# Attention and MLP on one core: the first batch's steps in another order, with zero products between them

## The chip, the cores and the metric

The kernel runs on one core of a Trainium2 chip. The metric is the device time of one execution in microseconds (us). Before the change it is 412.58 us, the median of three runs (412.34 to 412.92).

A core has five engines that each work through their own instructions in program order and wait for one another by semaphores: TensorE (PE, matrix products, with its weight loads PEld beside it), VectorE (DVE), ScalarE (ACT, exponentials and other activations), GpSimd (POOL) and SyncE (SP, which here only issues DMAs). DMAs are also issued by POOL and ACT. All DMAs of the core share 16 DMA engines.

## The reference

```python
rmsnorm = lambda x, g: x / np.sqrt(np.mean(x * x, -1, keepdims=True) + 1e-6) * g
q_n, k_n = rmsnorm(q, g_q), rmsnorm(k, g_k)          # q, k, v: 8 x 12 x 448 x 64
scores = q_n @ k_n.transpose(0, 1, 3, 2) / 8
attn = exp(scores - max) / (sum + 1e-9)
x = (attn @ v).transpose(0, 2, 1, 3).reshape(3584, 768)
out = gelu_tanh(x @ w_in) @ w_out                    # w_in 768 x 2048, w_out 2048 x 768
```

Eight batches; inputs and output are float32, the kernel multiplies in bfloat16.

## The kernel before, in words

Each batch has 12 heads, worked in six pairs (`hp` 0 to 5), and three chunks `c` of two pairs each (`hp = 2c + j`). For each chunk the raw q and k come in by DMA (`loads(b, c)`, lines 114 to 149, issued by SP: two for q, four for k). Then squares (`square`, L174), sums of the squares (`total`, L203, DVE), the inverse root (`rsqrt`, L209 and L212, an Ln and an Exp on ACT), the product with it (`normed`, L226), a transpose on PE (`trans`, L238 for q and L245 for k) and a copy out of PSUM (`place_q` L251, `place_k` L257). Scores are k against q (L324, and L310 for the 64 left-over keys of two pairs together), the exponential is on ACT (L331), and from it come on PE the row sums (`o` with `ones`) and the products with v (`ox` with `vb`, `vr`), both L370. The sums are turned into inverses on DVE (`recip_in`, `recip`, `recip_out`, L377 to L385), and `pair_x` (L395) gives the attention's output. The first layer of the MLP is `mm1` (L412, tiles `hh` and `h`) with `gelu` (L421), the second is `mm2` (L441).

From the second batch on, one batch's second-layer products fill PE between the next batch's attention steps. In the first batch there is nothing to fill with, and what every engine does in which order is written out by hand as a string `FRONT` (L761) that `front(step)` (L669) carries out one step after another. Every engine keeps the string's order for its own instructions. The steps are named so (`:A`, `:D`, `:P` say ACT, DVE or POOL):

- `sq0` to `sq5`, `sk0` to `sk5`: squares of pair number i; `tq`, `tk`: their sums; `rs`: Ln and Exp; `nq`, `nk`: products; `tpq`, `tpk`: transposes; `cq`, `ck`: copies out.
- `gcol`, `shift`: the gains g_q g_k and the constant under the exponential, with four zero products.
- `s0` to `s20`, `e0` to `e20`: 21 tiles of scores and their exponentials. Tile 3 (and 10, 17) holds the left-over keys of both pairs of a chunk, so it needs both pairs' q and k. Two PSUM buffers hold scores, three after step `U`.
- `sa`, `sb`: row sums in two halves; `xa`, `xb`: products with v in two halves; `st`, `rc`, `rb`, `xt`: inverses and `pair_x`.
- `y`n: n zero products of 224 columns; `z`m: m zero products of 448 columns into pair 0's sum bank, which its sum later overwrites. Both call `idle` (L214). The string before has one `y3` and no `z`.
- `v0` to `v2`: DMAs of batch 0's v from POOL (`v0` is the large part `vb`, `v1` and `v2` the left-over keys `vr`); `V` the same of batch 1; `w0` to `w3`: four parts of w_in; `o0` to `o3`: four parts of w_out, all from POOL. `L11`: `loads(1, 1)`, and so on.
- Batch 1's own preparation has capitals: `Sq`, `Sk`, `Tq`, `Tk`, `Rs`, `Nq`, `Nk` (`Nk01`: chunk 0, j 1), `Tp`, `Cq`, `Ck`.
- `mb`, `ma`, `mc`, `md`: first-layer products of batch 0; `g`: their gelu. `GELU` and `EXP` load activation tables.

Ahead of `FRONT` stand `loads(0, 0)`, `loads(0, 1)`, `loads(0, 2)`, `loads(1, 0)` (L604 to L608) and 20 zero products of 448 columns.

Of the kernel before, what the change touches and what calls it, by code (L numbers as in the profile page):

```python
# [8 lines left out]
F32 = mybir.dt.float32  # L9
# [7 lines left out]
def kernel(  # L17
# [12 lines left out]
    B, H, S, D = q.shape  # L30
# [8 lines left out]
    P = 112  # L39
    NQ = S // P  # L40
# [70 lines left out]
    def head(c, j):  # L111
        return 2 * c + HP * j

    def load_q(b, c):
        t = rawqk.tile([P, CH, NQ, D], F32, tag="rawq", name="rawq")
        raws["q", b, c] = t
        return [
            lambda j=j: nc.sync.dma_start(  # L118
                t[:, 2 * j:2 * j + 2],
                q[b, head(c, j):head(c, j) + 2].rearrange("h (p t) d -> p h t d", t=NQ),  # L120
            )
            for j in range(2)
        ]
# [481 lines left out]
    nc.scalar.preload_act_table_set(EXP_SET)  # L605
    loads(0, 1)
    loads(0, 2)
    loads(1, 0)  # L608
    nc.vector.memset(eps, 1e-6)
    nc.vector.memset(ones, 1.0)  # L610
    nc.vector.memset(rows, 1.0)
# [57 lines left out]
    def front(step):  # L669
        what, _, eng = step.partition(":")  # L670
        name, i = what.rstrip("0123456789"), what[len(what.rstrip("0123456789")):]
        i, eng = int(i or 0), ENG.get(eng)
        c, j = i // 2, i % 2
        n = name[-1]
        if name in ("sq", "sk"):
            square(0, c, n, eng, ("pair", j))
        elif name in ("tq", "tk"):
            total(0, c, n, j)
        elif name == "rS":
            rsqrt(0, i, slice(0, 30))  # L680
        elif name == "rs":
            rsqrt(0, c, slice(14 * j, 14 + 16 * j))
        elif name in ("nq", "nk"):
            normed(0, c, n, j, eng)
        elif name in ("tpq", "tpk"):
            tps[n, i] = trans(0, i, n, ps_t_tiles, name)
        elif name == "cq":
            place_q(0, i, tps["q", i], eng)
        elif name == "ck":
            place_k(0, i, tps["k", i], eng)  # L690
        elif name == "U":
            third()
        elif name == "gcol":
            gains()
        elif name == "shift":
            shifts()
        elif name == "s":
            exps[i] = scores(0, *TILES[i])
        elif name == "e":
            exps[i]()  # L700
        elif name == "z":
            hp, m = divmod(i, 100)
            if hp not in sums_at:
                sums_at[hp] = bank()
            idle(m, sums_at[hp][:, :S])
        elif name == "y":
            idle(i, ps_m.tile([128, 512], F32, tag="mm", name="w")[:, :S // 2])
        elif name in ("sa", "sb"):
            pair_products(0, i, 0, sums_at.get(i), "ab".index(n))
        elif name == "su":  # L710
            pair_products(0, i, 0, sums_at.get(i))
        elif name == "xp":
            pair_products(0, i, 1, ps_m.tile([128, 512], F32, tag="mm", name="ox"))
        elif name == "st":
            recip_in()
        elif name == "rc":
            recip()
        elif name == "rb":
            recip_out(i)
        elif name in ("xa", "xb"):  # L720
            pair_products(0, i, 1, ps_m.tile([128, 512], F32, tag="mm", name="ox") if n == "a" else None,
                          "ab".index(n))
        elif name == "xt":
            pair_x(0, i)
        elif name == "v":
            load_v(0, i)
        elif name == "w":
            w_in_part(i, NW)
        elif name == "V":
            load_v(1, i)  # L730
        elif name == "o":
            w_out_part(i // 2, slice(i % 2 * nf // 2, (i % 2 + 1) * nf // 2))
        elif name == "L":
            loads(*divmod(i, 10))
        elif name in ("Sq", "Sk"):
            square(1, i, n, eng)
        elif name in ("Tq", "Tk"):
            total(1, i, n)
        elif name == "Rs":
            rsqrt(1, slice(0, 2))  # L740
        elif name in ("Nq", "Nk"):
            normed(1, i // 10, n, i % 10, eng)
        elif name == "Tp":
            tps["Q", i] = trans(1, i, "q", ps_o, "o")
            tps["K", i] = trans(1, i, "k", ps_m, "mm")
        elif name in ("Cq", "Ck"):
            (place_q if n == "q" else place_k)(1, i, tps[n.upper(), i], eng)
        elif name in ("GELU", "EXP"):
            nc.scalar.preload_act_table_set(EXP_SET if name == "EXP" else GELU_SET)
        elif name == "mb":  # L750
            mm1(0, [0, 1], [i], act=False)
        elif name in ("ma", "mc", "md"):
# [22 lines left out]
    for step in FRONT.split():
        front(step)
# [159 lines left out]
```

## Time and profile before

| what | value |
|---|---|
| median of three runs | 412.58 us |
| the profiled execution's own time | 413.83 us |
| its span, first to last instruction | 412.1 us |
| mean granted TensorE clock | 0.992 of full speed |
| busy share of the span: PE, DVE, ACT, POOL | 98%, 67%, 72%, 32% |
| chain of waits that ended last, PE's share | 95% |
| read from memory, written | 45.61 MB, 11.01 MB |

A row of the timeline gives the start in us from the span's start, the duration, the engine, the line, the operation, the tile written and those read, sizes, and how many instructions of the kind stand in a row. In brackets is the engine's idle time before it and whose signal ended it. A row of stretches gives for a window the busy us (and number of instructions) of PE, PEld, DVE, ACT and POOL, then the granted clock, the busy share of the DMA engines and GB/s. A row of a group gives busy us, mean ns of one, idle time before. Squares of batch 0 are written into the space of the tile `g`, so they appear as `g<-rawq` and `g<-rawk`. Matmul durations include the drain of the array, so a product's price is read from the distance of two starts.

### The profile page before, as it was taken

How to read it: one execution, taken by the hardware profiler on the slowest of the kernel's cores; microseconds unless marked ns; L12 is line 12 of the kernel's file. 1: busy time of each engine (PE TensorE's matmuls, PEld its weight loads, DVE VectorE, ACT ScalarE, POOL GpSimd, SP SyncE). 2: the span in 40 equal slices, each digit the busy share in tenths (PEclk: the TensorE clock that was granted, in tenths of full speed). 3: DMA queues.
4: the chain of work that ended last, by engine and by line, in shares of the span. 5: the costliest groups of instructions: out<-in, count | busy, mean ns of one | idle time of the engine just before them, and what ended most of it. 6: DMA issues, size and time to landing. Idle time of an engine off the chain costs nothing.

```text
span 412.1 us, 10085 instructions
## 1 busy us (share of the span) xinstructions
PE 403.7 (98%) x4207; PEld 243.5 (59%) x4207; DVE 274.3 (67%) x454; ACT 296.2 (72%) x398; POOL 131.8 (32%) x144
## 2 busy tenths in 40 slices
PE   8799999999999999999999999999999999999996
PEld 3344555566655666557655666556655575556664
DVE  4899739899899638884678747786488633783010
ACT  5797987969988587767977778785976558774300
POOL 7689000234500942037500745019310460000000
PEclk9699999999999999999999999999999999999999
DMA  8999995999981689229981399616991161210022
GB/s 191 227 235 228 203 196 141 227 227 192 213 145 38 139 176 207 66 52 176 222 140 41 78 203 171 136 40 145 171 145 40 23 112 40 72 46 2 2 77 78
DMA packets 97870, 54.21 MB, mean 132 GB/s; under 512 B 63776, under 2 KB 94368, under 8 KB 97824
## 3 DMA queue, kind: packets, MB, share of 16 engines
q1 hardware_dynamic: 71392, 41.69, 43.4%
q0 software_dynamic: 26112, 11.80, 22.5%
q8 instruction: 33, 0.54, 0.6%
q10 hardware_dynamic: 320, 0.07, 0.1%
q14 instruction: 13, 0.11, 0.1%
HBM read 45.61 MB, written 11.01 MB: 137 GB/s over the span
## 4 chain that ended last, share of the span: by engine, by line
PE 95%; SPq 2%; DMA 1%; DVE 0%; ACT 0%; issue 0%; ACTq 0%; DVEq 0%
PE o L441 36%; PE hh L412 31%; PE o L370 11%; PE sc L324 8%; PE h L412 5%; PE sc L310 1%; DMA rawq<-in_q_dram 1%; PE ox L370 1%; SPq L143 1%; SPq L118 1%; SPq L136 1%; PE tp L245 0%; PE o L477 0%; PE tp L238 0%; ACT ex L331 0%
## 5 line engine op out<-in xcount | busy, mean ns | idle before, releaser
L441 PE MATMUL o<-wout,g 128*64 128x384 bf16 (+1 forms) x1648 | 160.6, 327 | 0.0
L331 ACT ACTIVATE ex<-sc,shift 128x896 bf16<-128x896 f32 x144 | 136.1, 1011 | 1.3 <-PE sc L324 1.3
L412 PE MATMUL hh<-xT,win 128*64 128x448 bf16 (+1 forms) x1260 | 133.8, 353 | 0.0
L441 PEld LDWEIGHTS <-g 128*64 128x64 bf16 (+1 forms) x1648 | 96.2, 109 | 58.3 <-issue 14.8
L412 PEld LDWEIGHTS <-win 128*64 128x64 bf16 (+1 forms) x1440 | 95.4, 109 | 49.9 <-issue 3.2
L421 ACT ACTIVATE g<-hh 128x896 bf16<-128x896 f32 x56 | 50.1, 919 | 44.5 <-PE hh L412 44.4
L203 DVE TENSOR_REDUCE ss<-sq 128x14 f32<-128x896 f32 (+4 forms) x45 | 47.9, 1080 | 32.4 <-ACT sq L186 19.9
L454 ACT COPY osb<-o 128x384 f32<-128x384 f32 x50 | 24.2, 483 | 47.8 <-PE o L441 47.8
L788 POOL COPY mark<-es 1x1 bf16<-1x1 bf16 x8 | 1.8, 225 | 162.9 <-DVE es L345 158.5
L377 DVE STREAM_TRANSPOSE st<-o 128x448 f32<-128x448 f32 x48 | 31.1, 648 | 23.6 <-PE o L370 23.2
L324 PE MATMUL sc<-qT,kT 64*128 64x448 bf16 (+1 forms) x372 | 39.6, 360 | 1.7 <-DVE kT L264 1.3
L345 DVE TENSOR_TENSOR es<-ex 128x896 bf16<-128x896 bf16 x42 | 26.8, 637 | 12.0 <-ACT ex L331 12.0
L226 POOL TENSOR_TENSOR nrmq<-rawq,rinv 112x512 bf16<-112x512 f32 x33 | 34.0, 1043 | 0.0
L226 POOL TENSOR_TENSOR nrmk<-rawk,rinv 128x512 bf16<-128x512 f32 (+1 forms) x33 | 31.1, 957 | 4.2 <-ACT rinv L212 4.2
L385 DVE STREAM_TRANSPOSE rb<-rc 128x448 f32<-128x448 f32 x48 | 31.0, 645 | 1.6
L370 PE MATMUL o<-ex,vb 128*64 128x448 bf16 x252 | 30.9, 352 | 0.0
L279 DVE TENSOR_SCALAR kT<-kT,gcol 128x896 bf16<-128x896 bf16 x19 | 21.1, 1108 | 11.7 <-DMA kT<-nrmk 11.7
L343 DVE TENSOR_TENSOR es<-es,exr 64x896 bf16<-64x896 bf16 x42 | 25.9, 617 | 2.4 <-ACT exr L331 1.0
L345 DVE TENSOR_TENSOR es<-es,ex 128x896 bf16<-128x896 bf16 x42 | 25.5, 608 | 2.3 <-ACT ex L331 0.3
L395 DVE TENSOR_TENSOR xT<-o,rb 128x448 bf16<-128x448 f32 x42 | 25.8, 615 | 1.4 <-PE o L370 0.9
L188 POOL TENSOR_TENSOR sq<-rawq 112x1024 f32<-112x1024 f32 x9 | 17.0, 1893 | 28.4 <-DMA rawq<-in_q_dram 25.0
L324 PEld LDWEIGHTS <-kT 64*128 64x128 bf16 (+1 forms) x372 | 10.9, 99 | 24.6 <-issue 18.1
(83 smaller groups left out, 349.4 us busy)
## 6 DMA issues: line engine op xcount, KB each, us to landing
rawq<-in_q_dram SPq DMA_DIRECT2D x48, 224.0 KB, 4.4
rawk<-in_k_dram SPq DMA_DIRECT2D x48, 192.0 KB, 4.6
vb<-in_v_dram POOLq DMA_DIRECT2D x8, 576.0 KB, 10.1
win<-in_moe_w_in_dram POOLq DMA_DIRECT2D x4, 768.0 KB, 14.1
wout<-in_moe_w_out_dram POOLq DMA_DIRECT2D x4, 768.0 KB, 20.4
out_dram<-osb SPq DMA_DIRECT2D x7, 336.0 KB, 4.3
out_dram<-osb SPq DMA_DIRECT2D x8, 288.0 KB, 2.7
out_dram<-osb SPq DMA_DIRECT2D x8, 240.0 KB, 2.6
```

The costliest lines, as they stand in the source:

```text
L203: nc.vector.reduce_sum(stat(ssq[b % 3], b, c, n, j), view(n, sqs[n, b, c], j), axis=AX.X)
L226: eng.tensor_mul(dst.rearrange("p t a d -> p a t d"), view(n, raws[n, b, c], j), r.to_broadcast(list(r.shape) + [D]),)
L324: nc.tensor.matmul(sc[o, a, :S], kT[r, c, 4 * j + t, o], qT[b][r, hp], start=True, stop=True,)
L331: nc.scalar.activation(dst, sc[:, :, :S], AF.Exp, scale=scale, bias=shift)
L343: nc.vector.tensor_add(es[p], es[p], exrs[b, hp // 2][p])
L345: nc.vector.tensor_add(es, ex[:, 0] if t == 1 else es, ex[:, t])
L370: nc.tensor.matmul(o[a * D:(a + 1) * D], w(a), e[:, a], start=(i == 0), stop=(i + 1 == len(steps)),)
L377: nc.vector.transpose(oas["st"].rearrange("p a b -> p (a b)"), oas[0])
L385: nc.vector.transpose(oas["rb", hp], oas["rc"].to_broadcast([128, S // 32, 32]))
L412: nc.tensor.matmul(h[i * m:(i + 1) * m, j, :S], win[:, c // 2 + NCH * (c % 2), f * 128 + i * m:f * 128 + (i + 1) * m], xT[b][:, c], start= ...
L421: nc.scalar.activation(g[:, fs[0]:fs[0] + len(fs), (b % 2) * S:(b % 2 + 1) * S], hs1[fs[0]][:, :, :S], AF.Gelu_apprx_tanh)
L441: nc.tensor.matmul(o[j * m:(j + 1) * m, :HD], g[:, f, i * 128 + j * m:i * 128 + (j + 1) * m], wout[:, f, half * HD:(half + 1) * HD], start ...
```

## The change

Three things change. `loads(1, 0)` is no longer issued ahead of `FRONT` but at a step `L10` in it, and a new step `H10` sets one element of its q tile to zero on POOL, for which the DMA into that tile has to wait. The string `FRONT` is another: squares and products change engine (`sq0` from ACT to POOL, `sq1` from POOL to DVE, `sk2` from ACT and `sk3` from POOL to DVE, `sq2` from ACT to POOL, `sq4` from POOL to ACT, `nq0` and `nk0` swap DVE and POOL, `cq1` from DVE to ACT; in batch 1 `Sk1`, `Sk2`, `Sq2` from ACT to POOL and `Sq0` from POOL to ACT, where it stands ahead of `e20`), `v1`, `v2` and `v0` come earlier on POOL, `w0` later, and there are more zero products: `y4`, `z5`, `y3`, `y1`, `y5`, `y1`, `y4`, `y1`, `z2`. What is computed stays the same.

```diff
+    def raw_q(b, c):
+        if ("q", b, c) not in raws:
+            raws["q", b, c] = rawqk.tile([P, CH, NQ, D], F32, tag="rawq", name="rawq")
+        return raws["q", b, c]
+
     def load_q(b, c):
-        t = rawqk.tile([P, CH, NQ, D], F32, tag="rawq", name="rawq")
-        raws["q", b, c] = t
+        t = raw_q(b, c)
...
     loads(0, 2)
-    loads(1, 0)
...
+        elif name == "H":
+
+            eng.memset(raw_q(*divmod(i, 10))[:1, 0, 0, :1], 0.0)
...
     FRONT = """
-        sq0:A sk0:P gcol tq0 tk0 sq1:P rs0 sk1:A nq0:P v1 nk0:D shift tq1 tk1 sq2:A tpq0 tpk0 v2
-        v0 sk2:A rs1 sq3:A cq0:D ck0:D tq2 s0 e0 y3 s1 nk1:D nq1:D L11 e1 tpk1 tpq1 s2 sk3:P w0
-        tq3 tk2 rs2 e2 ck1:D cq1:D s3 e3 sa0 s4 sk4:P tk3 nq2:D nk2:D rs3 tpk2 tpq2 s5 sb0 tk4
-        ck2:D cq2:D nq3:D st0 e4 nk3:P e5 s6 sk5:P L12 e6 tpk3 tpq3 s7 e7 s8 sa1 s9 sb1 xa0 e8
-        sq4:P sq5:P w1 rc0 cq3:D rb0 ck3:D tq4 tk5 rs4 e9 xb0 s10 st1 xt0 rc1 rb1 tq5 e10 sa2
-        s11 e11 rs5 nk4:P nq4:P w2 nk5:P nq5:P xa1 xb1 sb2 s12 e12 s13 tpk4 tpq4 xt1 st2 ck4:D
-        cq4:D rc2 xa2 e13 rb2 sa3 xb2 s14 tpk5 tpq5 s15 e14 xt2 ck5:D cq5:D sb3 e15 U s16 s17
-        xa3 xb3 s18 w3 o0 Sk0:P e16 st3 rc3 rb3 e17 xt3 e18 s19 sa4 xa4 sb4 xb4 Tk0 st4 rc4 s20
-        mb0 mb1 mb2 mb3 sa5 e19 e20 o1 Sq0:P Sq1:P V0 rb4 GELU xt4 Tq0 xa5 sb5 xb5 st5 V1 V2 o2
-        o3 Sk1:A rc5 rb5 ma1 mc0 mc1 xt5 md0 ma2 md1 mc2 md2 Tq1 Tk1 g0 EXP md3 Rs0 g1 Nk00:D
-        Nq11:D Nq00:D Tp0 md4 Cq0:A g2 Sq2:A g3 Nk10:D Nk01:D Nq01:D Ck0:D Tp1 md5 Sk2:A Tq2 Tk2
-        Nk11:D Nq10:D Ck1:A g4 Cq1:A g5 md6 md7 g6 g7 md8 g8
+        sq0:P sk0:P tq0 tk0 gcol rs0 sq1:D sk1:A v1 v2 tq1 nq0:D nk0:P tk1 shift tpq0 tpk0 y4 v0
+        rs1 sq3:A ck0:D cq0:D s0 e0 s1 z5 y3 nk1:P sk2:D nq1:D H10:P sq2:P e1 tpk1 s2 y1 tpq1 y5
+        y1 y4 tq3 tk2 e2 ck1:D sk3:D tq2 L10 cq1:A rs2 s3 e3 tk3 nk2:D nq2:D rs3 y1 z2 s4 sa0 s5
+        sb0 tpq2 tpk2 nq3:D st0 ck2:D cq2:D e4 sk4:P nk3:P e5 s6 sq5:P w0 w1 sk5:P e6 sq4:A tpk3
+        tpq3 s7 sa1 s8 sb1 xa0 e7 e8 s9 xb0 rc0 tk4 rb0 tq4 ck3:D cq3:D st1 xt0 e9 rs4 s10 tk5
+        tq5 rc1 rb1 L11 L12 e10 s11 xa1 sa2 rs5 e11 nq4:P nk4:P nq5:P nk5:P xb1 sb2 s12 tpq4
+        tpk4 xt1 e12 st2 ck4:D cq4:D s13 xa2 sa3 e13 rc2 rb2 s14 tpq5 tpk5 s15 xb2 e14 ck5:D
+        cq5:D xt2 sb3 e15 U s16 s17 xa3 xb3 s18 Sk0:P w2 w3 e16 st3 rc3 rb3 e17 xt3 e18 s19 sa4
+        sb4 xa4 s20 xb4 mb0 mb1 mb2 Tk0 st4 rc4 mb3 sa5 e19 Sq0:A o0 Sq1:P o1 V0 V1 Sk1:P V2 rb4
+        e20 GELU o2 xt4 Tq0 sb5 xa5 xb5 st5 Sk2:P o3 Sq2:P rc5 rb5 mc0 ma1 xt5 md0 mc1 ma2 md1
+        mc2 md2 Tk1 Tq1 g0 EXP md3 Rs0 g1 Nk00:D Nq00:D Nq01:D Tp0 md4 Nk10:D Nk11:D Nk01:D g2
+        g3 Cq0:D Ck0:A Tp1 md5 Nq11:D Tq2 Cq1:D Nq10:D Tk2 Ck1:A g4 g5 md6 md7 g6 g7 md8 g8
 """
```

## The prediction

> **What bounds the kernel now.** I read the page's slices first, then the stretches by clock, then the order of time on each engine. In the slices TensorE (PE) stands at nine tenths from about 15 us to the last slice; what can move the end is how early its dense work begins.
>
> ```profile
> 10.00:15.00 5.00, 2.31 (x18) 1.06 (x19) 5.00 (x11) 3.50 (x8) 3.69 (x4) 0.90 1.37 219
> 15.00:20.00 5.00, 5.00 (x29) 1.79 (x28) 4.21 (x10) 4.32 (x7) 2.74 (x3) 0.50 1.34 235
> 20.00:25.00 5.00, 4.59 (x41) 2.03 (x41) 4.42 (x10) 4.66 (x7) 4.10 (x5) 0.92 1.20 233
> ```
> The last columns are granted clock, DMA share and GB/s. PE is busy for 2.31 of 5 us in the first stretch, and the clock falls to half for the next: 0.90, 0.50 and 0.92 put the half clock from 14.0 to about 20.8 us. The DMA engines are full all along.
>
> PE in order of time (start, duration, line, what; in brackets the idle time before it):
> ```profile
> 1.16 6.91 PE L217 MATMUL w<-zeros 128*128 128x448 bf16 x20 [1.16 <-DVE zeros L81]
> ...
> 8.13 0.93 PE L217 MATMUL w<-zeros 128*128 128x448 bf16 x4
> ...
> 9.10 0.33 PE L245 MATMUL tp<-ident,nrmk 128*128 128x128 bf16 x3
> 10.73 0.36 PE L324 MATMUL sc<-qT,kT 64*128 64x448 bf16 x2 [1.30 <-DVE kT L264]
> 11.02 0.46 PE L217 MATMUL w<-zeros 128*128 128x224 bf16 x3
> ...
> 13.36 0.37 PE L238 MATMUL tp<-ident,nrmq 112*128 112x112 bf16 x4 [1.05 <-DVE nrmq L226]
> ...
> 14.80 0.88 PE L310 MATMUL sc<-qT,kT 64*64 64x448 bf16 x4 [0.78 <-DVE kT L264]
> ...
> 36.34 0.55 PE L370 MATMUL o<-ex,ones 128*64 128x448 bf16 x4
> 36.72 0.55 PE L370 MATMUL ox<-ex,vb 128*64 128x448 bf16 x4
> 37.20 7.74 PE L412 MATMUL hh<-xT,win 128*128 128x448 bf16 x40
> 44.82 0.37 PE L238 MATMUL tp<-ident,nrmq 112*128 112x112 bf16 x4
> ...
> 47.52 0.36 PE L238 MATMUL tp<-ident,nrmq 112*128 112x112 bf16 x4
> ```
> PE waits for VectorE (DVE) until 14.8; from 37.20 the 40 products of the first layer take 0.19 us each (7.74 us without a gap). Zero products raise the clock too: the first twenty average 0.35 us, those at 8.13 take 0.23 with their drain.
>
> ScalarE (ACT), the 21 exponentials of batch 0 and their neighbours:
> ```profile
> 10.54 0.61 ACT L186 ACTIVATE g<-rawq 112x512 f32<-112x512 f32 x1
> 11.13 1.91 ACT L331 ACTIVATE ex<-sc,shift 128x896 bf16<-128x896 f32 x2
> 14.39 0.31 ACT L209 ACTIVATE lg<-ss,eps 128x14 f32<-128x14 f32 x1 [1.36 <-DVE ss L203]
> ...
> 14.85 0.99 ACT L331 ACTIVATE ex<-sc,shift 128x896 bf16<-128x896 f32 x1
> 15.74 1.00 ACT L331 ACTIVATE exr<-sc,shift 128x896 bf16<-128x896 f32 x1
> ...
> 17.11 1.01 ACT L331 ACTIVATE ex<-sc,shift 128x896 bf16<-128x896 f32 x1
> ...
> 32.25 2.82 ACT L331 ACTIVATE ex<-sc,shift 128x896 bf16<-128x896 f32 x3
> ...
> 46.47 1.06 ACT L186 ACTIVATE sq<-rawq 112x1024 f32<-112x1024 f32 x1
> ```
> The same engine between 10 and 35 us, one group:
> ```profile
> L331 ACT ACTIVATE ex<-sc,shift 128x896 bf16<-128x896 f32 x18 | 17.3, 1006 | 1.3 <-PE sc L324 1.3
> ```
> One exponential follows another by 0.89 us (14.85 to 15.74), an rs step puts in 0.46 (14.39 to 14.85). e3 starts at 15.74, e20 ends at 35.07. Between them ACT is full but for 1.3 us in which scores came late, most of it at half clock. So batch 0 is set by when e3 starts and by ACT behind it. PE is then 1.3 us behind ACT (its last sums start at 36.34).
>
> **The change part by part.** DVE and GpSimd (POOL) need rows of their own:
> ```profile
> 9.96 0.38 DVE L255 COPY qT<-tp 128x448 bf16<-128x448 bf16 x1
> 10.26 0.41 DVE L264 TENSOR_SCALAR kT<-tp,gcol 128x384 bf16<-128x384 bf16 x1
> ...
> 11.78 1.53 DVE L226 TENSOR_TENSOR nrmq<-rawq,rinv 112x512 bf16<-112x512 f32 x1
> 13.23 1.13 DVE L203 TENSOR_REDUCE ss<-g 112x8 f32<-112x512 f32 x2
> ...
> 15.57 0.67 DVE L226 TENSOR_TENSOR nrmq<-rawq,rinv 112x512 bf16<-112x512 f32 x1
> 16.17 0.54 DVE L226 TENSOR_TENSOR nrmk<-rawk,rinv 128x384 bf16<-128x384 f32 x1
> ...
> 43.01 0.56 DVE L226 TENSOR_TENSOR nrmk<-rawk,rinv 128x384 bf16<-128x384 f32 x1 [1.62 <-ACT rinv L212]
> ```
> ```profile
> 8.43 1.48 POOL L159 DMA_DIRECT2D vr<-in_v_dram  x2
> 9.90 1.06 POOL L153 DMA_DIRECT2D vb<-in_v_dram  x1
> 11.71 1.04 POOL L188 TENSOR_TENSOR g<-rawk 128x512 f32<-128x512 f32 x1 [0.76 <-DMA rawk<-in_k_dram]
> ...
> 30.42 1.70 POOL L188 TENSOR_TENSOR sq<-rawk 128x896 f32<-128x896 f32 x1
> ...
> 33.01 3.75 POOL L188 TENSOR_TENSOR sq<-rawq 112x1024 f32<-112x1024 f32 x2
> ```
> The same DVE product takes 0.67 us at 15.57 and 1.53 at 11.78, while POOL's square of 11.71 runs; POOL lost nothing. Two-input products of DVE and POOL shut each other out, and here the one that stood waiting went ahead of DVE's next product. The Trainium skill, "SBUF — State Buffer", section "Who interferes with whom", says that a DVE tensor_tensor with both inputs in SBUF contends with GpSimd's reads and that the later one blocks fully. The trace agrees (1.53 against 0.67); the rule speaks against this change, which gives both engines more such products.
>
> *Before e0.* The first square goes to POOL (1.04), sq1 to DVE (no DVE square is in the trace: 0.60 by the product's spacing from 15.57 to 16.17, at most POOL's 1.04), and tq1 now comes ahead of nq0. PE's zero products still hold the first transposes until 9.10, so this is hidden: nq0 on DVE waits for POOL's nk0 and ends near 8.3. What DVE no longer has ahead of cq0 is one reduction, 0.60: I get ck0, cq0 ending at 10.2 and s0 at 10.27 instead of 10.73. But sq3 stands ahead of e0 on ACT and waits for its load. With 0.61 for sq3, e0 starts at about 10.85 instead of 11.13.
>
> *v sooner.* The issues (1.48 and 1.06) move from 8.43 and 9.90 to about 5.4 and 7.7. Landing of k's and q's loads here, the q half for sq3 (issued 5.34), v's large part, and the last k of batch 1:
> ```profile
> DMA to landing us min/median/max: 4.8/4.8/4.8
> ```
> ```profile
> DMA to landing us min/median/max: 10.7/10.7/10.7
> ```
> ```profile
> DMA to landing us min/median/max: 11.5/11.5/11.5
> ```
> sq3's load lands at 10.14; v's small pieces now share its last microsecond, which I price at 0.1 (0 if they start as late after the issue as the 3 us that other loads need, 0.7 if they take every other packet from 7 on). v's large part landed at 20.6; its first reader xa0 moves from 22.84 to about 20.4. I take no wait; a landing at 21.5 would cost about 0.5 at e9, 0 if v gains its two microseconds.
>
> *DVE from 10.2 to e3.* Behind cq0 stand sk2 (new on DVE), nq1, tq3, tk2, ck1, sk3 (new), tq2, then rs2 on ACT, which is queued ahead of e3. sk2 waits for POOL's nk1 (9.62 to 10.66) and ends at 11.1. POOL's sq2 waits by then and goes first, as at 11.71, so nq1 ends at 12.5 (unblocked 11.7). tq3 and tk2 (1.1 by the 13.23 row), ck1 (0.4), sk3 (0.60), tq2 (0.6) give 15.2; rs2 starts at 15.26, e3 at 15.73. That is where it was. The two squares taken over by DVE eat what was won before; ACT waits about 1.2 us ahead of rs2 with cq1 hidden in it. **Below and above:** 14.87 if DVE keeps the turn at 11.1, 16.5 if POOL's sk4 also gets in ahead of sk3.
>
> *Zero products.* y4, z5, y3, y1, y5, y1, y4, y1, z2: 23 short ones against 3, and 7 long ones. At 0.1 us (11.02 row: three to 11.41) and 0.19 they add 2.0 + 1.3 = 3.3 us to PE, all ahead of s4, where PE would stand waiting: s2 waits for e0's buffer (11.8) and z5, y3 end at 11.9; s3 waits for ck1 and cq1 (14.0) and the ten end at 13.9. Cost 0.1; if a wait is shorter by d than I think, the rest of d is on the path. What they buy is the clock: between 10.6 and 14.0 PE had three pairs of scores, three short ones and two sets of transposes, some 1.3 us of 3.4; with the fillers it has 2.8. The Trainium skill, "TensorE: Matmul & The Clock Gate", section "Why this matters for your kernels", asks only that no gap exceeds about 3 us; here the clock fell with no gap over 1.30 us, so the trace decides. By that page the fillers would be useless.
>
> *From e3 to e20 at full clock.* The 1.3 us of late scores go. ACT gets new work: sq4 (0.59 by 10.54 to 11.13), and Sq0 (some 0.94 of its 1.06 before the next starts) ahead of e20. With e4 at 17.1: 17 exponentials by 0.89 = 15.1, rs4 and rs5 0.92, sq4 0.59, Sq0 0.94, drain 0.1: e20 ends at 34.8 instead of 35.07. PE, which no longer lags, waits for it: sb5, xa5, xb5 are three times four products, 0.38 each (36.34 to 36.72): 36.05 instead of 37.20. **Sum: -1.15 us** at the start of the dense stretch.
>
> *Batch 1.* H10 writes one element on POOL; done at about 10.8, while SP reaches the load that waits for it at 11.61:
> ```profile
> 11.61 0.59 SPq L118 DMA_DIRECT2D rawq<-in_q_dram  x1
> ```
> So it costs nothing unless POOL is 0.8 us late; behind it on SP stand only batch 1's loads. w0 is issued near 19 instead of 12.7 and should land near 29, with mb0 at 32. Sk1, Sk2, Sq2 move from ACT to POOL. ACT has room there, so no gain; for their price see the second rival.
>
> The profiled execution took 413.83 us, 412.1 of it span; the median shown is 412.58. I take the shift from the median: 412.58 - 1.15 = **411.4 us**. About 0.2% (0.83 us) is what a measurement of this kernel can tell from no change.
>
> **The rivals.** *DVE keeps its turn at 11.1.* Then e3 is at 14.87, 0.86 sooner: 410.5. For it: POOL has H10 between nk1 and sq2. Against: the 11.78 row.
> *Squares of batch 1 shut DVE out (slower).* Nk00 hangs on g0 and so on md0, which comes after 12 instead of 14 first-layer products: 43.01 - 1.15 - 0.38 = 41.5. DVE's six products Nk00 to Nk01 then run to 44.8 (0.5 to 0.6 each), and PE reaches the transposes that need them at 43.7 and 46.4 (44.82 and 47.52, less 1.15, rounded). POOL's Sk2 takes 1.70 and, one DMA issue later, Sq2 1.88. If both fall between those products, Nk01 ends at 44.8 + 3.6, near 48.3, against 46.4: PE stands some 1.8 us (1.9 less what the transposes of q hide), the sum is +0.65: 413.2. The point: Sk2 starting between 41.2 and 43.1. It waits for a load that landed 11.5 us after its issue near 32; w0 being late brings it sooner, which makes this serious. Outside that stretch it costs 0 to 0.9.
> *The clock falls all the same.* From 14.0 to 17.4 PE has some 1.85 us of work in 3.4 (s3, s4, s5 0.65, sa0 and sb0 0.76, fillers 0.45) while ACT waits for rs2. A half clock after that gives back about the 1.0 us of score waits: 412.4.
>
> **How the numbers follow.** Forecast (411.4) 0.36; DVE's turn 0.17; squares 0.24; clock 0.13; a wait that I do not see (v's landing, a load behind v) 0.10. Faster by over 0.2% holds three quarters of the forecast, all of DVE's turn and some rest: 0.48. Slower holds half of the squares (when the first transposes are late too), half of the clock's and of the unseen: 0.23; the remainder 0.29. The range reaches below to all of ACT's waits gone (e0 at 10.85, then 21 by 0.89, four rs, cq1 0.4, sq4, Sq0 and the drain: e20 at 33.4 and 2.5 us in all, 410.1) and above to the squares with sk4's 0.6 beside: 410.0 to 413.8.
>
> **What would show it.** Clock 1.00 from 10 to 25 us; e3 within 0.3 of 15.7 and rs2 waiting for DVE; a DVE product of over 1.3 us near 11; no score wait on ACT from e4 to e20; the row of 40 products at 36.0. Wrong would be: e3 near 15 or past 16.3; an idle time of PE before line 238 near 46; xa0 waiting for v.

## The result, and the profile after

The changed kernel takes 415.63 us (median of 8 runs, 414.28 to 418.39) against 412.88 for the kernel before in the same session (8 runs, 412.34 to 413.32): 2.75 us slower by the medians, a ratio of 1.0071 [1.0053, 1.0089], which is 2.2 to 3.7 us. The profiled execution took 415.65 us, 413.8 of it span. Line numbers up to L460 are those of before plus 4 (L203 is L207, L412 is L416), those of the w_in and w_out issues plus 3 (L636 is L639).

First the stretches of after, which answer to the three of before; the last columns are clock, DMA share and GB/s:
```profile
10.00:15.00 5.00, 4.86 (x40) 2.82 (x38) 5.00 (x8) 3.79 (x6) 1.73 (x3) 1.00 1.36 217
15.00:20.00 5.00, 3.03 (x28) 1.39 (x27) 4.98 (x8) 4.94 (x9) 4.10 (x4) 1.00 1.21 232
20.00:25.00 5.00, 4.71 (x46) 2.03 (x45) 4.71 (x11) 4.28 (x8) 3.23 (x4) 1.00 1.17 215
```
The clock is 1.00 all through, as forecast; PE is at 3.03 of 5 us in the second stretch all the same: it is now waiting.

The profiled execution does not stand for all eight in this. In four of them the mean granted clock was 0.999 or more, and they took 414.28 to 415.65 us (median 414.85, 1.97 above before). In the other four it was 0.992 to 0.996, which at half clock makes a spell of some 3 to 7 us (an estimate from 413 us), and they took 415.61 to 418.39 (median 416.92).

The chain of ACT in order of time:
```profile
10.47 0.63 ACT L190 ACTIVATE g<-rawq 112x512 f32<-112x512 f32 x1 [1.18 <-DMA rawq<-in_q_dram]
11.01 2.79 ACT L335 ACTIVATE ex<-sc,shift 128x896 bf16<-128x896 f32 x3
...
14.95 0.31 ACT L213 ACTIVATE lg<-ss,eps 128x14 f32<-128x14 f32 x1 [0.74 <-DVE ss L207]
...
15.41 0.99 ACT L335 ACTIVATE exr<-sc,shift 128x896 bf16<-128x896 f32 x1
...
20.68 2.97 ACT L335 ACTIVATE ex<-sc,shift 128x896 bf16<-128x896 f32 x3 [0.62 <-PE sc L328]
...
34.65 1.02 ACT L335 ACTIVATE ex<-sc,shift 128x896 bf16<-128x896 f32 x1
```
e0 (11.01) and e3 (15.41) are within 0.4 of the forecast and rs2 waits for DVE, as it said. But e20 ends at 35.67 instead of 34.8. The first piece lost behind e3 is ahead of e7, where scores come late by 0.62 although the clock is full. DVE, POOL and PE say why:
```profile
9.77 1.06 DVE L192 TENSOR_TENSOR g<-rawk 128x384 f32<-128x384 f32 x1
10.76 1.52 DVE L230 TENSOR_TENSOR nrmq<-rawq,rinv 112x512 bf16<-112x512 f32 x1
...
16.01 2.77 DVE L230 TENSOR_TENSOR nrmq<-rawq,rinv 112x512 bf16<-112x512 f32 x2
...
19.27 0.37 DVE L268 TENSOR_SCALAR kT<-tp,gcol 128x384 bf16<-128x384 bf16 x1
19.57 0.37 DVE L259 COPY qT<-tp 128x448 bf16<-128x448 bf16 x1
...
42.44 1.06 DVE L230 TENSOR_TENSOR nrmk<-rawk,rinv 128x384 bf16<-128x384 f32 x1 [1.40 <-ACT rinv L216]
43.43 3.65 DVE L230 TENSOR_TENSOR nrmq<-rawq,rinv 112x512 bf16<-112x512 f32 x2
47.00 1.75 DVE L230 TENSOR_TENSOR nrmk<-rawk,rinv 128x384 bf16<-128x384 f32 x3
```
```profile
10.42 1.31 POOL L192 TENSOR_TENSOR g<-rawq 112x512 f32<-112x512 f32 x1
15.76 1.03 POOL L192 TENSOR_TENSOR g<-rawk 128x384 f32<-128x384 f32 x1 [4.03 <-DMA rawk<-in_k_dram]
16.92 1.31 POOL L230 TENSOR_TENSOR nrmk<-rawk,rinv 128x512 bf16<-128x512 f32 x1
...
41.41 1.67 POOL L192 TENSOR_TENSOR sq<-rawk 128x896 f32<-128x896 f32 x1 [1.53 <-DMA rawk<-in_k_dram]
43.04 0.94 POOL L639 DMA_DIRECT2D wout<-in_moe_w_out_dram  x1
44.01 1.91 POOL L192 TENSOR_TENSOR sq<-rawq 112x1024 f32<-112x1024 f32 x1
```
```profile
19.69 0.38 PE L249 MATMUL tp<-ident,nrmk 128*128 128x128 bf16 x4 [1.47 <-POOL g L192]
19.99 0.36 PE L242 MATMUL tp<-ident,nrmq 112*128 112x112 bf16 x4
20.28 0.36 PE L328 MATMUL sc<-qT,kT 64*128 64x448 bf16 x2
```
From 9 us on there are three places where a two-input product of DVE lies beside one of POOL: sk2 and nq1 at 9.77 and 10.76 (1.06 and 1.52, where such a product takes 0.6 to 0.7 alone), nq2 and nq3 at 16.01 (2.77 for the two), and batch 1's products at 42.44 and 43.43 (1.06, and 3.65 for two) beside Sk2 and Sq2. At the first, POOL runs `nk1` and then sq2: `nk1` also moved from DVE to POOL, which the list of changes ahead of the prediction leaves out (so it does for `Cq0`, `Ck0` and `Cq1`). At the second, pair 2's copies out of PSUM (19.27 and 19.57) stand on DVE behind nq2 and nq3, and PE's next transposes and e7's scores (20.28) follow them; POOL's square, which the row at 19.69 names as the release, is not read by these transposes. PE shows the price of the third:
```profile
37.00 7.81 PE L416 MATMUL hh<-xT,win 128*128 128x448 bf16 x40
46.53 0.37 PE L242 MATMUL tp<-ident,nrmq 112*128 112x112 bf16 x4 [1.72 <-DVE nrmq L230]
...
57.66 2.63 PE L445 MATMUL o<-wout,g 128*64 128x384 bf16 x30
```
PE stands for 1.72 us before its first transposes of batch 1, "an idle time of PE before line 238 near 46". From the row at 57.66 the rest of the span takes 356.1 us, as in before; over all the profiles of this study it is 355.8 to 357.4. So the loss is made ahead of 57 us.

### The profile page after: what moved, and what is told of

Same layout as the page of the kernel before. It is cut to its first block, busy times and chain, and to the rows that moved or that the text cites. A ratio compares the mean times of both kernels' runs of the same rounds, so it can differ in the third digit from the quotient of the medians.

```text
span 413.8 us, 10136 instructions
## 1 busy us (share of the span) xinstructions
PE 404.3 (98%) x4230; PEld 244.8 (59%) x4230; DVE 282.4 (68%) x456; ACT 293.5 (71%) x394; POOL 136.4 (33%) x147
## 3 DMA queue, kind: packets, MB, share of 16 engines
HBM read 45.61 MB, written 11.01 MB: 137 GB/s over the span
## 4 chain that ended last, share of the span: by engine, by line
PE 61%; issue 15%; POOL 10%; DVE 6%; DMA 3%; SPq 2%; ACT 1%; ACTq 0%; POOLq 0%; DVEq 0%
PE o L445 24%; PE hh L416 18%; PE o L374 7%; PE sc L328 5%; POOL nrmk L230 4%; POOL nrmq L230 3%; PE h L416 3%; DMA rawq<-in_q_dram 2%; DVE ss L207 1%; DVE nrmq L230 1%; PE ox L374 1%; DMA rawk<-in_k_dram 1%; DVE es L349 1%; POOL g L192 1%; PE sc L314 1%
## 5 line engine op out<-in xcount | busy, mean ns | idle before, releaser
L416 PE MATMUL hh<-xT,win 128*64 128x448 bf16 (+1 forms) x1260 | 133.9, 353 | 0.0
L416 PEld LDWEIGHTS <-win 128*64 128x64 bf16 (+1 forms) x1440 | 95.4, 109 | 50.0 <-issue 3.5
L207 DVE TENSOR_REDUCE ss<-sq 128x14 f32<-128x896 f32 (+4 forms) x45 | 47.9, 1080 | 27.6 <-ACT sq L190 16.8
L230 POOL TENSOR_TENSOR nrmk<-rawk,rinv 128x512 bf16<-128x512 f32 (+1 forms) x35 | 33.1, 960 | 1.0 <-ACT rinv L216 0.8
L230 POOL TENSOR_TENSOR nrmq<-rawq,rinv 112x512 bf16<-112x512 f32 x32 | 32.7, 1036 | 1.8 <-ACT rinv L216 1.8
L283 DVE TENSOR_SCALAR kT<-kT,gcol 128x896 bf16<-128x896 bf16 x19 | 22.7, 1193 | 12.0 <-DMA kT<-nrmk 12.0
L349 DVE TENSOR_TENSOR es<-es,ex 128x896 bf16<-128x896 bf16 x42 | 26.9, 639 | 2.3 <-ACT ex L335 0.3
```

The source lines that it names most:

```text
L207: nc.vector.reduce_sum(stat(ssq[b % 3], b, c, n, j), view(n, sqs[n, b, c], j), axis=AX.X)
L230: eng.tensor_mul(dst.rearrange("p t a d -> p a t d"), view(n, raws[n, b, c], j), r.to_broadcast(list(r.shape) + [D]),)
L349: nc.vector.tensor_add(es, ex[:, 0] if t == 1 else es, ex[:, t])
L416: nc.tensor.matmul(h[i * m:(i + 1) * m, j, :S], win[:, c // 2 + NCH * (c % 2), f * 128 + i * m:f * 128 + (i + 1) * m], xT[b][:, c], start= ...
```

## The experiments

**Theory A**: the loss comes from DVE and POOL shutting each other out, in two parts: sk2 on DVE holds up batch 0, and Sk2 and Sq2 on POOL hold up batch 1's products. **Rivals**: v's earlier loads take DMA time from loads that are waited for; the zero products are in the way, or are of use and hide more loss; Sq0 on ACT ahead of e20. Every diff is of words in the string `FRONT`, cut down to those around each edit; ratios are to the kernel before, run beside it.

**e1, e2, e3, e4: one part of the change undone each.** e1 puts Sk2 and Sq2 back on ACT, e2 issues v later, e4 does both, e3 leaves all zero products out but `y3`.
```diff
-xb5 st5 Sk2:P o3 Sq2:P rc5
+xb5 st5 o3 rc5
-g2 g3 Cq0:D
+g2 Sq2:A g3 Cq0:D
-md5 Nq11:D
+md5 Sk2:A Nq11:D
```
```diff
-sk1:A v1 v2 tq1 nq0:D nk0:P tk1
+sk1:A tq1 nq0:D nk0:P v1 v2 v0 tk1
-y4 v0 rs1
+y4 rs1
```
```diff
-tpk0 y4 v0
+tpk0 v0
-s1 z5 y3 nk1:P
+s1 y3 nk1:P
-s2 y1 tpq1 y5
-y1 y4 tq3
+s2 tpq1 tq3
-rs3 y1 z2 s4
+rs3 s4
```


> The changed kernel with batch 1's last two squares (Sk2, Sq2) on ACT again, where they stood before the change; nothing else differs. If the exclusion between GpSimd's squares (41.41 to 43.08 and 44.01 to 45.92 us in the changed kernel's profile) and VectorE's six products Nk00 to Nk01 makes the loss, the 1.72 us of idle time of TensorE ahead of the transposes at 46.53 goes, the six products take 3.4 us instead of about 6.3, and the time falls by 1.7 us or more, from 415.6 to 413.9 or below. If the loss comes from the first 37 us, the idle time may go but the time stays within 0.5 us of 415.6.

> The changed kernel with batch 0's v asked for after nk0 instead of ahead of it (v1, v2 about 7.5 instead of 5.2 us, v0 about 9.0 instead of 7.5). If the sooner v made the k load of pair 4 late (it landed at 15.7 us, 7.4 after its issue, against 13.1 before), it lands near 14.2, sk4 no longer holds nq2 up at 16.0, ACT's 0.62 us of waiting ahead of e7 goes, and the row of 40 first-layer products starts near 36.4 instead of 37.0. The stop at Nq00 stays or changes by its own timing, so the whole time falls by 0.3 to 0.8 us only. If v is not what delays that load, it lands at 15.5 or later and the row of 40 stays at 37.0.

> The changed kernel with only y3 of its zero products, as before the change. If the zero products hold the clock up, the granted clock falls to 0.5 for some 7 us between 14 and 21 us, scores reach ACT late (about 1 us in all between e4 and e20) and the time rises by 0.5 to 1.5 us. If they sit on the path instead, TensorE reaches its first real steps sooner, e2 comes up to 0.3 us earlier, and the time stays or falls by up to 0.3 us.

> Both edits of the first two: Sk2 and Sq2 on ACT and v asked for after nk0. If the port exclusion and the late load each cost what the profile shows (1.7 and 0.6 us), the time is 2.3 us or more below the changed kernel, 413.3 or lower, at about the level of the kernel before (412.9) or under it. If only one of the two counts, it stands where that one's own run stands.

Measured: e1 414.55 us, 1.0039 [1.0024, 1.0055], and PE has no idle time before the first transposes any more; e2 415.88, 1.0070 [1.0048, 1.0092]; e3 415.7, 1.0075 [1.0055, 1.0096]; e4 415.14, 1.0054 [1.0037, 1.0071]. The squares cost about 1.1 us: e1 falls between its two expectations, and e4, which was to reach 413.3, stands near e1.

v's place shows no gain either way, but e2 is not a clean test of it. As hoped, the k of pair 4 landed 5.8 us after its issue instead of 7.4, and ACT's wait ahead of e7 is gone. But the later issues of v bring POOL's `nk1` and sq2 later, and sk2 on DVE waits for both, so e3 comes at 16.81 instead of 15.41:
```profile
10.30 2.78 DVE L192 TENSOR_TENSOR g<-rawk 128x384 f32<-128x384 f32 x1
```
With v as early as in after, that k took 4.7 to 7.7 us in twelve profiles, so v's place does not fix it.

e1's profile shows what the zero products can cost. Its clock is at half from about 10.7 to 14.1 us. PE and ACT of e1:
```profile
10.96 2.05 PE L221 MATMUL o<-zeros 128*128 128x448 bf16 x5
...
44.75 0.36 PE L242 MATMUL tp<-ident,nrmq 112*128 112x112 bf16 x4
```
```profile
14.42 1.01 ACT L335 ACTIVATE ex<-sc,shift 128x896 bf16<-128x896 f32 x1 [1.72 <-PE sc L328]
```
The five products of `z5` take 2.05 us (1.12 in after), what stands behind them on PE is late, and ACT waits 1.72 us for e2's scores. e15's profile has the same (1.98 and 1.65). So the zero products do not always hold the clock, and when it falls ahead of them they stand in the way. The single times agree: where zero products were added, executions with a mean granted clock of 0.996 or less are slower than the others of the same kernel (by medians e6 415.53 against 412.53, e11 414.84 against 413.10, e13 417.29 against 415.25, e15 416.12 against 414.50). No experiment sets the fall of the clock by itself.

e3 looks as if the zero products were worth nothing, but its profile says more. PE of e3, then its second stretch:
```profile
38.40 7.81 PE L416 MATMUL hh<-xT,win 128*128 128x448 bf16 x40
46.76 0.37 PE L242 MATMUL tp<-ident,nrmq 112*128 112x112 bf16 x4 [0.55 <-DVE nrmq L230]
```
```profile
15.00:20.00 5.00, 4.49 (x28) 1.78 (x26) 4.27 (x10) 3.92 (x8) 3.09 (x4) 0.50 1.25 247
```
Without the zero products the clock is at half for 10 us and the row of 40 starts 1.40 later than in after (38.40 against 37.00), yet the transposes start only 0.23 later (46.76 against 46.53). Their start is set by POOL's squares; whatever the front wins or loses ahead of them is swallowed. While that collision stands, experiments on the front show little.

**e5, e6: the kernel before again, and with zero products.** e5 is the kernel before, e6 has `y4` behind `tpk0`, `z3 y3` behind `s1`, `y5` behind `tpk1`, `y1 y4` behind `s2` and `z2` behind `s3`.
```diff
-tpq0 tpk0 v2 v0
+tpq0 tpk0 y4 v2 v0
-s0 e0 y3 s1
+s0 e0 s1 z3 y3
-tpk1 tpq1 s2
+tpk1 y5 tpq1 s2 y1 y4
-s3 e3
+s3 z2 e3
```


> The kernel before, unchanged, to have a second profile of it. If the first profile (span 412.1 us) stood for the usual execution, the row of 40 products starts within 0.2 us of 37.20. If the front of that one execution was a late one, the row starts up to 1 us sooner (near 36.2) with a span near 411.1, and about 1 us of the gain that was expected had been in the median already.

> The kernel before with added zero products alone, put where TensorE waited in its profile: y4 behind tpk0, z3 and y3 behind s1, y5 behind tpk1, y1 and y4 behind s2, z2 behind s3. If the clock is what they buy and batch 0 hangs on it, the granted clock stays at 1.00, ACT's 1.3 us of waiting for scores goes and the time falls by about 1 us, from 413.0 to 412.0. If ACT is full behind e3 whatever the clock, or if they delay real steps, the time stays within 0.4 us or rises.

Measured: e5 412.63 (one run), e6 412.55, 0.9994 [0.9978, 1.0010]. Rows of e5: two of ACT and PE that the prediction had at 15.74 and 37.20, then two of DVE and POOL that it had at 11.78 and 11.71:
```profile
14.77 1.00 ACT L331 ACTIVATE exr<-sc,shift 128x896 bf16<-128x896 f32 x1
```
```profile
35.60 7.74 PE L412 MATMUL hh<-xT,win 128*128 128x448 bf16 x40
```
```profile
11.65 0.68 DVE L226 TENSOR_TENSOR nrmq<-rawq,rinv 112x512 bf16<-112x512 f32 x1
```
```profile
12.35 1.03 POOL L188 TENSOR_TENSOR g<-rawk 128x512 f32<-128x512 f32 x1 [1.45 <-DMA rawk<-in_k_dram]
```
The execution of before from which the prediction was made (413.83 us) was a late one: in an execution of 412.63 us e3 is 0.97 and the row of 40 is 1.60 sooner. Most of the 0.97 is again DVE and POOL shutting each other out. In the first execution POOL's square of pair 3's k ran into nq1 (1.53 us); in e5 that k lands later, the square starts at 12.35, and nq1 is done in 0.68. And a held clock (e6: 1.00 from 10 to 25 us) gains nothing that can be told: the interval is 0.9 us faster to 0.4 slower.

**e7, e8: Sq0 and sk2.** e7 is e1 with `Sq0:P`; e8 is e7 with sk2 on ACT behind rs1.
```diff
-e19 Sq0:A o0
+e19 Sq0:P o0
-v0 rs1 sq3:A
+v0 rs1 sk2:A sq3:A
-nk1:P sk2:D nq1:D
+nk1:P nq1:D
```


> The changed kernel with Sk2 and Sq2 on ACT as in the first of these runs (414.55 us) and Sq0 on GpSimd as before the change, so that it no longer stands ahead of e20. If the 0.94 us that Sq0 takes on ACT is on the path, e20 ends that much sooner, the row of 40 products starts near 36.2 instead of 37.1 and the time is near 413.6. If TensorE or the tail of batch 0 on VectorE sets that row instead, it starts at 36.8 or later and the time stays within 0.3 us of 414.55.

> As the last one, and sk2 on ACT again (behind rs1) instead of VectorE. In the changed kernel sk2 on VectorE ran from 9.77 to 10.83 with GpSimd's nk1 in its way, and nq1 behind it until 12.28. If that chain sets e3, nq1 ends 0.5 to 0.9 us sooner, e3 starts near 14.8 instead of 15.4 and the time falls by about 0.6 us more, to 413.0 or lower. If e3 then waits for something else (the two loads of the second pair, tpq1, TensorE's zero products), the time stays.

Measured: e7 415.02, 1.0063 [1.0038, 1.0088], neither of its expectations (its profile is that of its slowest execution, 417.91, with half clock from about 20.7 to 24.1 us); e8 414.57, 1.0042 [1.0025, 1.0060]. In e8 the row of 40 starts at 35.73, but Sk1 is late on POOL behind Sq0, Rs0 waits 0.88 for DVE and PE 0.44 and 0.40 for what follows. Taking Sq0 off ACT only moves the wait.

**e9, e10, e11: halves of the string.** e9 has after's string up to `s18` and then before's, e10 the reverse, e11 is e9 with sk2 on ACT behind rs1.
```diff
-xa3 xb3 s18 Sk0:P w2 w3 e16
+xa3 xb3 s18 w2 w3 o0 Sk0:P e16
...
```


> The string of the changed kernel up to s18, the string of before from there on (batch 1's squares on the engines and at the places of before, no Sq0 ahead of e20, no square on GpSimd among Nk00 to Nk01). If the loss is all in the part behind s18, the row of 40 products starts near 36.0, TensorE stands nowhere behind it, and the time is that of before (413.0) or lower. If the new front loses by itself (late k load of pair 4 after v, more work on VectorE and ACT), the row starts at 36.8 or later and the time stays 0.7 us or more over 413.0.

> The other half: the string of before up to s18 and that of the changed kernel from there on (Sk1, Sk2, Sq2 on GpSimd, Sq0 on ACT ahead of e20). By the exclusion of VectorE and GpSimd TensorE stands ahead of the transposes near 46 whatever the front does, at about 46.5 as in the changed kernel, where the row of 40 products ended 1.7 us before: the time rises by 1.3 us or more over 413.0. If the squares cost only in company with the new front, the time is within 0.5 us of 413.0.

> As the new front with the old rest, and sk2 on ACT behind rs1 instead of on VectorE. With sk2 on ACT the row of 40 products stood at 35.7 in an earlier run (37.1 without), but Sk1 on GpSimd, made late by Sq0, held batch 1's rs back there by 0.9 us. With the old rest that wait goes: time near 412.7, at or under the kernel before. If the row's 35.7 was a chance of that execution, the time is that of the run beside it without this edit.

Measured: e9 414.51, 1.0036 [1.0021, 1.0052]; e10 413.14, 1.0000 [0.9992, 1.0009]; e11 413.32, 1.0013 [1.0000, 1.0026]. The new front alone costs 1.5 us, about 1 of it sk2's engine. The new rest alone shows no cost: the squares on POOL miss the products. POOL of e10 (the release named there is a wrong guess; the last k was issued at 34.5 and took 11.2 us to land), and its PE:
```profile
45.87 2.05 POOL L188 TENSOR_TENSOR sq<-rawk 128x896 f32<-128x896 f32 x1 [5.46 <-DVE qT L255]
```
```profile
44.19 0.36 PE L238 MATMUL tp<-ident,nrmq 112*128 112x112 bf16 x4
```

**e12: what might beat both.** e6 with `v1` at the head of POOL's queue, ahead of the large part of v.
```diff
-sq0:A sk0:P gcol
+sq0:A sk0:P v1 gcol
-nq0:P v1 nk0:D
+nq0:P nk0:D
```


> The kernel before with the zero products of the earlier run (412.55 us) and v1 asked for behind sk0 instead of behind nq0, so that v's large part follows 0.7 us sooner. In that run's profile TensorE waited 0.77 us for v's large part at 21.6 us. If this wait is on the path, 0.5 to 0.7 us go: near 412.0, a clear gain on before. If ACT or another load sets the end of batch 0, the time stays near 412.5.

Measured: 412.40 us, 0.9983 [0.9972, 0.9995]: the one version that is shown to be ahead of both kernels, by 0.65 us of the kernel before. The wait of 0.77 us for `vb` that e6 had at 21.60 is gone, but that e12 is ahead of e6 is not shown.

**e13, e14: w0 alone.** The prediction had said that the late w0 brings the last k sooner. e13 is after with w0 early, e14 is e10 with w0 late.
```diff
-H10:P sq2:P e1
+H10:P sq2:P w0 e1
-sq5:P w0 w1
+sq5:P w1
```
```diff
-s2 sk3:P w0 tq3
+s2 sk3:P tq3
-sq4:P sq5:P w1
+sq4:P sq5:P w0 w1
```


> The changed kernel with w0 issued on POOL behind sq2 (about 13 us) instead of behind sq5 (19.6 us). Theory A (the late w0 lets batch 1's last k load be issued at 27.2 and land at 41.4, inside DVE's block of products): the last k is issued after 30 us, Sk2 on POOL starts past 44 or so, TensorE does not stand before Tp0 or stands under 0.6 us, 414.4 to 414.9 (the 415.6 of the change less the 1.1 that moving both squares to ACT gave). Rival B (the late Sq0 and o parts on POOL, or the k tiles coming free early, put the squares there and w0 has no part in it): Sk2 stays at 41 to 42.5, the wait of 1.1 to 1.7 us stays, 415.4 to 415.9.

> The order of before up to s18 and that of after behind it (413.14), with w0 moved from behind sk3 to behind sq5. Theory A: the last k is issued 3 to 5 us sooner, Sk2 on POOL starts between 41 and 43, TensorE stands 1 us or more before Tp0 or Tp1, 413.9 to 414.6. Rival B: Sk2 stays past 45, no such wait, 412.9 to 413.4.

Measured: e13 415.68, 1.0074 [1.0048, 1.0100]; e14 414.25, 1.0033 [1.0022, 1.0045]. POOL and PE of e14:
```profile
38.36 1.68 POOL L188 TENSOR_TENSOR sq<-rawk 128x896 f32<-128x896 f32 x1
...
41.99 1.91 POOL L188 TENSOR_TENSOR sq<-rawq 112x1024 f32<-112x1024 f32 x1
```
```profile
44.98 0.37 PE L238 MATMUL tp<-ident,nrmq 112*128 112x112 bf16 x4 [1.50 <-DVE nrmq L226]
```
w0 alone, moved later in e10, brings Sk2 from 45.87 to 38.36, Sq2 with it into DVE's products, and 1.50 us of idle PE. The other direction failed. SP and POOL of e13:
```profile
31.47 1.46 SPq L147 DMA_DIRECT2D rawk<-in_k_dram  x2
```
```profile
41.36 1.67 POOL L192 TENSOR_TENSOR sq<-rawk 128x896 f32<-128x896 f32 x1 [2.05 <-DMA rawk<-in_k_dram]
```
In after the last k was issued at 29.3, took 12.0 us to land, and POOL squared it at 41.41; in e13 it was issued at 32.3, took 8.9, and POOL squared it at 41.36. A late w0 is enough to make the collision but isn't needed for it in the new front. What else there fixes the landing (w2 is issued at 29.03 in e13 and at 24.14 in e10) is open.

**e15, e16: both parts.** e15 is after with sk2 on ACT behind rs1; e16 has Sk2 and Sq2 on ACT (as e1) beside.
```diff
-v0 rs1 sq3:A
+v0 rs1 sk2:A sq3:A
-nk1:P sk2:D nq1:D
+nk1:P nq1:D
```


> The changed kernel with sk2 on ACT behind rs1 and nothing else. If the front's loss and the collision simply add: 415.6 less 1.2 (what the same edit gave in the kernel with the new front alone) = 414.4. If the collision's end is set by the landing of the last k and not by the front: TensorE stands longer before Tp0 (2.5 us and more), Tp0 stays at 46.5 to 46.8 and the time is 415.2 to 415.7.

> The changed kernel with sk2 on ACT behind rs1, Sk2 on ACT behind md5 and Sq2 on ACT behind g2. If both losses are removed: 413.2 to 413.6, as the kernel with the new front alone and sk2 on ACT (413.32); the clock at 1.00 and no wait before Tp0. If something of the rest of the change costs too (Sq0 on ACT ahead of e20, Sk1 on POOL): 413.9 or more.

Measured: e15 414.99 (412.32 to 417.51), 1.0056 [1.0035, 1.0077], too wide to tell the two expectations apart; e16 413.13, 1.0010 [0.9998, 1.0021]. Three squares back on ACT take back 2.5 of the 2.75 us. Some 0.7 of this is that ten of e16's eleven executions kept the clock (0.998 or more) and only four of after's eight; among those that kept it the medians are 413.06 and 414.85, 1.8 us apart. DVE and PE of e16:
```profile
14.96 0.68 DVE L230 TENSOR_TENSOR nrmq<-rawq,rinv 112x512 bf16<-112x512 f32 x1
16.10 0.77 DVE L230 TENSOR_TENSOR nrmq<-rawq,rinv 112x512 bf16<-112x512 f32 x1 [0.46 <-ACT rinv L216]
...
41.09 1.29 DVE L230 TENSOR_TENSOR nrmq<-rawq,rinv 112x512 bf16<-112x512 f32 x2
```
```profile
35.17 7.81 PE L416 MATMUL hh<-xT,win 128*128 128x448 bf16 x40
42.82 0.36 PE L242 MATMUL tp<-ident,nrmq 112*128 112x112 bf16 x4
```
The products that took 2.77 and 3.65 in after take 0.68 and 0.77, and 1.29. PE goes from the row of 40 to the transposes without a gap, and the row is 1.83 sooner than in after. It is 0.43 sooner than in e5 too, and still e16 is not faster than before: the rest from the second layer's first products (at 54.18) takes 357.3 us, with a wait of PE for DVE of 0.81 us at 255 that the profiles of before and after do not have.

**e17, e18: what is left.** e17 is e16 with Sq0 behind e20 and the table load; e18 is e17 with `y3` as its only zero products.
```diff
-e19 Sq0:A o0
+e19 o0
-GELU o2
+GELU Sq0:A o2
```


> The kernel with sk2, Sk2 and Sq2 on ACT (413.13), and Sq0 on ACT moved from ahead of e20 to behind it and the table load. If ACT's own work is what still sets the first row of 40 products: the 0.95 us that Sq0 takes ahead of e20 go, 412.1 to 412.4, the row of 40 near 34.3. If Sq0 then comes late for batch 1 (its reduction holds VectorE ahead of xt5, or Rs0 waits): 412.8 to 413.6, with a wait of TensorE for xT or of ACT ahead of Rs0.

> The same kernel with one group of zero products (y3) in place of nine. If the clock that the others hold buys time once no product of VectorE is held up: half clock for 3 to 10 us between 10 and 25 us, waits of ACT for scores, 0.6 to 1.5 us slower than the same kernel with them. If such a spell stays hidden as in the kernel before: within 0.3 of it.

Measured: e17 415.03, 1.0051 [1.0032, 1.0070]; e18 415.46, 1.0050 [1.0036, 1.0065]. DVE and PE of e17:
```profile
35.63 1.22 DVE L207 TENSOR_REDUCE ss<-sq 112x16 f32<-112x1024 f32 x1 [1.58 <-ACT sq L190]
```
```profile
35.50 2.07 PE L416 MATMUL hh<-xT,win 128*128 128x448 bf16 x10
39.15 5.83 PE L416 MATMUL hh<-xT,win 128*128 128x448 bf16 x30 [1.58 <-DVE xT L399]
```
Sq0's sum stands on DVE ahead of pair 5's inverses, so PE waits 1.58 for its last attention output: the second expectation, and dearer than it said.

Sq0's price ahead of e20 can be read all the same. The first ten of the row of 40 start at 35.50 in e17, 20.55 behind e3 (14.95). In e16, with Sq0 ahead of e20, the row is 20.55 behind e3 (35.17 and 14.62), and in e8, with Sq0 on POOL, 20.55 too (35.73 and 15.18). Yet e20 ends 19.23 us behind e3 in e16 and 18.3 in the other two. PE is busy for 5.00 of 5 us from 25 to 30 and from 30 to 35 in all three: its own work sets the row, not e20, and Sq0 ahead of e20 costs the row nothing.

e18 shows half clock from about 12 to 19 us and 0.80 of late scores in its profile, but its ratio can't be told from e17's.

## Why the prediction was wrong

It forecast 411.4; the time is 415.63, outside the range. By its own steps:

- **"That is where it was" and "Sum: -1.15 us".** This step failed first. e3 at 15.74 and the row of 40 at 37.20 were those of one late execution; in e5 they stand at 14.77 and 35.60, and e10 and e14, with the old front, have e3 at 14.28 and 14.81. So e3 at 15.41, close to the forecast 15.73, is against e5 a loss of 0.64 and not a draw, and the forecast 36.05 for the row of 40 was 0.45 later than e5's. Taking the shift from the median after summing against a profile 1.25 us above it counted gains that the median already had.
- **DVE from 10.2 to e3.** Mechanism and sizes right: sk2 1.06, nq1 1.52, rs2 waiting for DVE. That sk2's place costs is borne out by e3's start: 15.41 to 16.81 in the eight profiles of the new front with sk2 on DVE, 14.62 to 15.18 in five of the six with it on ACT (e15, with half clock on its zero products, has 16.60).
- **"From e3 to e20 at full clock".** e20 ends 20.3 us behind e3 instead of 19.1. What the step did not see is that one product more on DVE moves nq2 past a late landing of pair 4's k, into POOL's square and nk3: 2.77 us for two products. The row of 40 follows e3 by 21.59 us, against 20.55 in e1, e8, e15, e16 and e17: a price of 1.04. It is in part chance, for it stands in after and e7 alone, where that k took 7.4 and 7.7 us to land. In e13, with sk2 on DVE too, POOL squares it at 14.02, nq2 and nq3 take 0.68 and 0.69, and e20 ends 19.2 behind e3.
- **"PE, which no longer lags, waits for it".** This failed as well, with the 0.94 for Sq0: PE is full from 25 to 35 us and does not wait for e20 (e8, e16, e17). The sum's 20.32 us from e3 to the row of 40 (36.05 less 15.73) is near the 20.55 of those runs by luck.
- **Squares of batch 1 shut DVE out.** The rival (0.24) came in: Sk2 at 41.41 (its point: 41.2 to 43.1), 1.72 us idle (it said 1.8), Tp0 at 46.53. Shown by e1. That the sizes agree is partly luck, for it had PE stand ahead of the second transposes, and PE stood ahead of the first. Its point was too narrow: in e14 Sk2 comes at 38.36, and Sq2 makes the collision. "w0 being late brings it sooner" holds in e14 and not in e13. Its 413.2 was too low because its sum stood on the -1.15. The Trainium skill, "SBUF — State Buffer", section "Who interferes with whom", says that the later of two such operations blocks fully, and the trace agrees for Nk00 at 42.44: 1.06 us beside Sk2 against 0.56 in before. Of the two products of 3.65 us, 1.29 without POOL's squares, the first started at 43.43, ahead of Sq2 (44.01), and was still done only behind it, which that rule does not give.
- **The sum put right.** Against e5 the row of 40 is 1.40 later, 0.64 of it at e3 and 0.76 behind, and PE's idle time 1.72 longer: 3.1 us, against 3.02 between the two executions and 2.75 between the medians. That the three squares are the cause of most of it is shown by e16. The rest of the loss lies with the executions whose clock fell, and is told from their times, not by an experiment.
- **Zero products.** The prediction counted 23 short ones; the string and the trace have 19, which make 1.6 us more instead of 2.0. Its price of 0.1 supposed that the clock holds. It held in the profiled execution and in half of the eight; in the others the rival that the clock falls all the same (0.13) came in, and their median is 2.07 us higher, against the 1.0 that it priced. A use is not shown: e6 gains nothing that can be told from none, and e18 loses nothing that can be told, though e3's and e18's profiles have the row of 40 later (1.40 than after's, 0.71 than e17's).
- **v sooner**, priced at 0.1: no gain or loss shown (e2, which also moved sk2). e0 came 0.16 later than forecast. **H10**: priced at nothing; not tried alone, but e11 and e16 hold it and stand at 1.0013 and 1.0010 of before.

## What to carry to other kernels

Sum a change against more than one execution, or first ask how far the profiled one lies from the median: a front that varies by 1.6 us hides or invents a gain of 1.15. Look at the granted clock of every execution, too, before calling a clock held. Count two-input products of DVE and POOL by stretch before moving one to the other engine; a product added ahead of a chain shifts all that follows into new overlaps. When several experiments show the same time, look for a later meeting point that swallows the difference, and remove that one first.

## What the runs showed of the hardware

- The spells of half clock in the profiles last 3.4 us (e1, e7, e15), 6.8 (before, e5, e14, e18) and 10.2 (e3, e10). The granted clock fell with no idle time of PE over 1.47 us ahead of it (e7); in after the same idle time (1.47, ahead of 19.69) went by without a fall. The Trainium skill, "TensorE: Matmul & The Clock Gate", section "Why this matters for your kernels", asks for no gap of PE over about 3 us; here the clock fell with none that long.
- One k load, issued at 8.3 to 8.7 us in all twenty profiles, landed 4.5 to 5.6 us later with the old front (six profiles) and 4.7 to 7.7 with the new one (fourteen). With the new one that moves POOL's square of pair 4 between 13.2 (e18) and 16.4 (e7).
- In after, e13, e14 and e15 a product of DVE that started while POOL issued a DMA between its two squares (43.43, 43.37, 41.17 and 42.59) was done only after the second square. In e2 sk2 started while POOL issued a DMA (10.30) and was done only after POOL's next two products, so the one that stands waiting does not always go next. Another product, at 7.15 in after, started while a product of POOL ran, with a DMA issue behind it; it took 0.93 and did get through. Why they differ is open.
